# Moving the maxima's score matmuls behind the first half of a slot's fill work

## The chip, the cores and the metric

The kernel runs on one core of one Trainium2 chip. That core has five engines, each of which works through its own list of instructions in order: TensorE (PE, matrix products; its weight loads are listed as PEld), VectorE (DVE), ScalarE (ACT), GpSimd (POOL) and SyncE (SP, which here starts the DMA transfers). An engine waits for another by semaphores. The metric is the device time of one execution in microseconds (us); lower is better. A run of the kernel before takes 732.83 us as the median of three (732.78 to 732.90).

## The reference

Inputs are float32. `x` is 2048 by 512, the attention has 32 heads of width 16 and a sliding window of 256 keys, the MLP has 1792 hidden features.

```python
def _A_ref(x, wqkv, wo):
    qkv = (x @ wqkv).reshape(B, S, 3, H, Dh).transpose(2, 0, 3, 1, 4)
    q, k, v = qkv[0], qkv[1], qkv[2]
    scores = einsum("bhqd,bhkd->bhqk", q, k) * (Dh ** -0.5)
    mask = (idx[:, None] - idx[None, :] >= 0) & (idx[:, None] - idx[None, :] < W)
    p = softmax(where(mask, scores, -1e9), axis=-1)
    return einsum("bhqk,bhkd->bhqd", p, v).transpose(0, 2, 1, 3).reshape(B, S, D) @ wo

def _B_ref(x, w1, b1, w2, b2):
    h = gelu(layernorm(x) @ w1 + b1)
    return h @ w2 + b2

xn = layernorm(A_x)
return A_x + _A_ref(xn, wqkv, wo) * silu(_B_ref(xn, w1, b1, w2, b2))
```

## The kernel before

**Stages.** The first 60 us or so load the inputs, normalise and transpose `x` and make the first projections. Then comes the attention loop, and then the rest of the MLP, the output projection and the gating. The change is in the attention loop.

**Slots.** Heads are taken in 8 groups of 4, and the 2048 rows in 16 blocks of 128, which gives 16 x 8 = 128 slots, numbered by `t`. In slot `t` three things are done for three different blocks, one behind the other:

- `prob_block` makes the probabilities of block `t`, in two passes (`p` = 1, then `p` = 0). PE writes scores into the PSUM tile `stb` (2 matmuls of 384 columns, one for each half of the array's rows), ACT takes the exponential of them into an SBUF tile `pt`, and POOL masks the edges of `pt` with `affine_select`. There is one `stb`, so the second pass waits until ACT has read the first.
- `max_block` finds the row maxima of block `m = t + 12`, which are subtracted later. PE writes 4 matmuls of 256 columns into the PSUM tile `xy` ("the maxima's scores", for the block itself and the one before it). DVE then runs `copy_predicated`, which replaces the masked half of the diagonal block by the scores of the block two before ("first-block scores", in the PSUM tile `zo`), and a `tensor_reduce` with max over `xy` into `mt`. The first-block scores of block `m + 1` are made at the end of slot `t` by `first_scores`: 4 matmuls of 128 columns into `zo[:, :, 0:256]`. For a group's first two blocks there is nothing two before, and the copy takes a constant (`negc`) in place of `zo`.
- `pv_step` multiplies the probabilities of block `t - 1` with the values: 24 short matmuls into `otb`, which is `zo[:, 1, 256:384]`. Then a copy takes `otb` to SBUF (`oraw`). ACT makes this copy in most slots, and DVE in the last slot of a job (below).

`zo` spans two PSUM banks of 512 columns: `zo[:, 0]` and `zo[:, 1]`. The first-block scores lie in both, and `otb` lies in the second one.

**Fills.** The projections that later slots need are cut into units that fill PE's time between these steps. `tandem(t0, t1, one, two)` takes two such jobs (12 steps each, or 24 of half the width) and runs them as pairs of matmuls into the two banks `fb`, over the slots `t0` to `t1`: a first phase up to `mid`, then a second with the array's rows exchanged, and a last few units in slot `t1`, from which the results are copied out by ACT. In this text a job's slot `t0` is its *first slot*, `mid` its *middle slot* and `t1` its *last slot* (the list `ends_pair`); `t1 + 1` is often the next job's first slot. Each unit is put into the first or the second half of a slot (`fills[t, 0]`, `fills[t, 1]`). The first unit of the second phase has a set dependency on the latest copy of `otb`:

```python
tc.add_manual_dep(r.ins, outs["copy"].ins.name, ORDER, reason="the banks change rows")
```

**Order.** Every engine but SP keeps the order in which the program records its instructions. The main loop records, for a slot: the pass `p` = 1, `max_block`, the first half's fills, planned extra work, the pass `p` = 0, the second half's fills, the first-block scores of the next slot's block, and `pv_step`:

```python
if 0 < t < end:
    prob_block(t // 16, t % 16, 1)
if t >= 0 and m < end:
    max_block(m // 16, m % 16, m not in IN_PLACE)
fill_in(t, 0)
```

Waits between engines are derived from which instruction reads or writes which tile, and are attached to the instruction that has to wait; what stands behind it in its engine's list waits with it.

Of the kernel before, what the change touches and what calls it, by code (L numbers as in the profile page):

```python
# [26 lines left out]
LEAD = 12  # L27
# [23 lines left out]
def mixer_kernel(ctx, tc, x, wqk, wv, wo, w1, b1, w2, b2, out):  # L51
# [25 lines left out]
    def load(pool, tag, src, name, shape=(P, 512)):  # L77
        t = pool.tile(list(shape), F32, tag=tag, name=name)
        nc.sync.dma_start(t, src)
        return t  # L80
# [63 lines left out]
    def run(steps):  # L144
        for step in steps:
            step()
# [13 lines left out]
    def open_slot(i):  # L160
        slots.append(bigp.tile([P, 2, 2, S], F32R, tag=f"qk{i}", name=f"qk{i}"))
# [123 lines left out]
    fills = {}  # L285
    IN_PLACE = (LEAD,)
# [171 lines left out]
    taken, ends_pair = set(), set()  # L458
# [32 lines left out]
    def tandem(t0, t1, one, two, mid=None, back=None):  # L491

        n = one[0]
        lo, hi = slice(0, 64), slice(64, P)
        mid = mid or max(1, (t0 + t1 + 1) // 2)
        most = n // 4

        def places(slots, last):  # L500

            last = min(most, n // (len(slots) + 1)) if last else 0
            cuts = [(n - last) * k // len(slots) for k in range(len(slots) + 1)]
            out = []
            for t, a, b in zip(slots, cuts, cuts[1:]):
                ahead = min(b - a, n // 3) if t < 16 * NQ - LEAD else min(b - a, max(most, (b - a + 1) // 2))
                out += [(t, 0)] * ahead + [(t, 1)] * (b - a - ahead)
            return out + [(t1, 0)] * last

        first, second = places(range(t0, mid), False), places(range(back or mid, t1), True)  # L510
        for phase, where in enumerate((first, second)):
            for i in range(n):
                flags = dict(start=(phase == 0 and i == 0), stop=(phase == 1 and i == n - 1), skip_group_check=True)
                def unit(i=i, phase=phase, flags=flags):
                    made = ((two if phase == 0 else one)[1](fb[1 - phase], i, hi, **flags),
                            (one if phase == 0 else two)[1](fb[phase], i, lo, **flags))
                    if phase == 1 and i == 0 and t0 < 16 * NQ - LEAD:
                        for r in made:
                            tc.add_manual_dep(r.ins, outs["copy"].ins.name, ORDER, reason="the banks change rows")
                fills.setdefault(where[i], []).append((unit, ()))  # L520
        fills.setdefault((t1, 0), []).append((one[2], (fb[0], t1, nc.scalar.copy)))
        if t1 >= 16 * NQ - LEAD:
            fills[t1, 0].append((two[2], (fb[1], t1, nc.vector.tensor_copy)))
            return
        ends_pair.add(t1)

        def copy(dst, src):
            outs["second"] = nc.scalar.copy(dst, src)
        fills.setdefault((t1, 1), []).append((two[2], (fb[1], t1, copy)))
# [15 lines left out]
    def first_scores(n, qb):  # L545

        slot = slots[n % 2]
        for p in range(2):
            for a in (1, 0):
                r = slice(64 * a, 64 * a + 64)  # L550
                nc.tensor.matmul(zo[:, a, P * p: P * (p + 1)], slot[r, 0, p, P * qb: P * (qb + 1)],
                                 slot[r, 1, p, P * (qb - 2): P * (qb - 1)], start=True, stop=True)

    def max_block(n, qb, ahead=False):

        slot = slots[n % 2]
        if qb % 4 == 0:
            mts[n, qb // 4] = small.tile([P, 2, 2, 4], F32, tag="mt", name=f"mt_{n}_{qb}")
        lo = max(qb - 1, 0)
        off = 128 * (lo + 1 - qb)  # L560
        for p in range(2):
            for a in (1, 0):
                r = slice(64 * a, 64 * a + 64)
                nc.tensor.matmul(xy[:, a, 256 * p + off: 256 * (p + 1)], slot[r, 0, p, P * qb: P * (qb + 1)],
                                 slot[r, 1, p, P * lo: P * (qb + 1)], start=True, stop=True)
        if qb >= 2 and not ahead:
            first_scores(n, qb)
        four = xy.rearrange("q a (p k) -> q a p k", p=2)
        outs["max"] = nc.vector.copy_predicated(
            four[:, :, :, 128:256], mask,  # L570
            neg if qb < 2 else zo[:, :, 0:256].rearrange("q a (p k) -> q a p k", p=2)),
        nc.vector.tensor_reduce(out=mts[n, qb // 4][:, :, :, qb % 4],
                                in_=four[:, :, :, off:256],
                                axis=AX.X, op=ALU.max, negate=True)
# [32 lines left out]
    def prob_block(n, kb, p):  # L607
        slot = slots[n % 2]
        w = min(384, S - P * kb)
        pt = pp.tile([P, 2, 384], F32, tag="pt", name=f"pt_{n}_{kb}_{p}")  # L610
        both = xy if p and 16 * n + kb + LEAD >= 16 * NQ else stb[0]
        for a in (1, 0):
            r = slice(64 * a, 64 * a + 64)
            nc.tensor.matmul(both[:, a, 0:w], slot[r, 1, p, P * kb: P * (kb + 1)],
                             slot[r, 0, p, P * kb: P * kb + w], start=True, stop=True)
        writers[n, kb, p] = [nc.scalar.activation(pt[:, :, 0:w], both[:, :, 0:w], AF.Exp, scale=DH ** -0.5)]
        select = nc.gpsimd.affine_select(out=pt[:, :, 0:P], in_=pt[:, :, 0:P], pattern=[[0, 2], [1, P]],
                                compare_op=ALU.is_ge, fill=0.0, base=0, channel_multiplier=-1)
        if w == 384:
            select = nc.gpsimd.affine_select(out=pt[:, :, 256:384], in_=pt[:, :, 256:384],  # L620
                                             pattern=[[0, 2], [-1, P]], compare_op=ALU.is_gt, fill=0.0,
                                    base=0, channel_multiplier=1)
        writers[n, kb, p].append(select)
        pts[(n, kb, p)] = pt
# [122 lines left out]
    def at(t, fn, *args):  # L747
        plan.setdefault(t, []).append((fn, args))
# [8 lines left out]
    ahead = load(pp, "pt", x[512: 640, :], "x_1_0")  # L757
# [144 lines left out]
           -10: [ln3[0][0], ln3[1][0], ln3[0][1], ln3[1][1], ln3[0][2], ln3[1][2]],  # L902
           -9: [ln3[2][0], ln3[3][0], ln3[2][1], ln3[3][1], ln3[2][2], ln3[3][2]]}

    def fill_in(t, half):
        now[:] = t, half
        run(delayed.pop((t, half), ()))
        for fn, args in fills.get((t, half), ()):
            fn(*args)

    end = 16 * NQ
    for t in range(-16, end + 1):
        m = t + LEAD
        if t == -5:
            open_slot(1)
            for k in range(4):
                at(-4 + k // 2 * 2, clear_part, k)
        if 0 < t < end:
            prob_block(t // 16, t % 16, 1)
        if t >= 0 and m < end:  # L920
            max_block(m // 16, m % 16, m not in IN_PLACE)
        fill_in(t, 0)
        for fn, args in plan.get(t, []):
            fn(*args)
        if 4 <= m < LEAD:
            max_block(0, m)
        if 0 <= t < end:
            prob_block(t // 16, t % 16, 0)
        fill_in(t, 1)
        if t == -1:  # L930
            early.close()
            stb.append(attn.enter_context(tc.tile_pool(name="ps_s2", bufs=1, space=PSUM)).tile(
                [P, 2, 512], F32, name="stb"))
            prob_block(0, 0, 1)
            fill_in(t, 2)
        if 0 <= m < 4:
            max_block(0, m)
        if t >= 0 and m + 1 < end and (m + 1) % 16 >= 2 and m + 1 not in IN_PLACE:
            first_scores((m + 1) // 16, (m + 1) % 16)
        if t >= 1:  # L940
            pv_step((t - 1) // 16, (t - 1) % 16)
        run(lns.get(t, ()))
        if 0 <= m < end and m % 4 == 3:
            max_rows(m // 16, m % 16 // 4, t)
        for fn, args in ends.get(t, []):
            fn(*args)
# [28 lines left out]
    for f in range(6, NF, 2):  # L975
        t = gp.tile([P, 2, 512], F32, tag="ohl", name=f"hr_{f}", bufs=4)
# [199 lines left out]
    for c in range(2):  # L1176
# [25 lines left out]
        ahead = 2 + c  # L1202
# [4 lines left out]
        for i in range(NF + 1):  # L1207
# [29 lines left out]
            k = i - o_from  # L1237
# [190 lines left out]
```

## Time and profile before

| | us |
|---|---|
| median of 3 runs | 732.83 |
| the profiled execution, its own time | 732.75 |
| its span, first to last instruction | 731.0 |
| PE busy in the span | 719.0 |
| DVE busy | 497.9 |
| ACT busy | 427.0 |
| POOL busy | 321.3 |

The span is what the profile shows; 732.75 - 731.0 = 1.75 us of the run's time lie around it. Busy time of PE is counted from the start of a matmul to a modelled end, and matmuls overlap in the array, so PE can be "busy" while it moves slower than it could. What a step costs is therefore read from the distance between the starts of two steps that follow each other on PE. In the rows below a step is named by the tile that it writes: `stb` (probability scores), `xy` (the maxima's scores), `fb` (a fill), `zo<-qk` (first-block scores), `zo<-pt,vt` (`pv_step`). All instructions carry the line L43, that of the helper that records them, so they are told apart by tile.

### The profile page before, as it was taken

The page shows a single profiled execution, that of the slowest core. Times are in us where ns is not written, and L with a number is a line of the kernel's source. Part 1 is how long each engine was busy: PE and PEld are TensorE (multiplying, and loading weights), DVE is VectorE, ACT ScalarE, POOL GpSimd, SP SyncE. Part 2 cuts the span into 40 slices and gives each one's busy share as a digit, 9 for nine tenths or more (in the row PEclk, how much of TensorE's full clock was granted, in tenths as well). Part 3 has the DMA queues.
Part 4 walks back from the last instruction along what each step waited for, and adds up shares of the span by engine and source line. Part 5 has one row for each costly group of instructions (what it writes and reads, how often), then busy time and mean ns, then how long its engine had stood idle before and what let it go on. Part 6 is the DMA issues. An engine that isn't in the chain of part 4 may idle for free.

```text
span 731.0 us, 19063 instructions
## 1 busy us (share of the span) xinstructions
PE 719.0 (98%) x7584; PEld 585.9 (80%) x7584; DVE 497.9 (68%) x733; ACT 427.0 (58%) x723; POOL 321.3 (44%) x681
## 2 busy tenths in 40 slices
PE   8999999999999999999999999999999999999997
PEld 7997777777778887777776788888888888888886
DVE  7886776877766777777882657446787855667833
ACT  7767777877777676888878735232343734541001
POOL 7444757767677665777877540203203000001102
PEclk9999999999999999999999999999999999999999
DMA  8324446877776733667624367347213312263701
GB/s 294 82 48 105 101 126 171 223 217 226 206 209 171 210 121 97 161 165 212 176 78 159 130 220 203 143 130 244 87 57 116 117 58 87 66 190 109 247 22 58
DMA packets 61528, 106.77 MB, mean 146 GB/s; under 512 B 12096, under 2 KB 12352, under 8 KB 61440
## 3 DMA queue, kind: packets, MB, share of 16 engines
q1 hardware_dynamic: 61440, 105.56, 49.3%
q8 instruction: 60, 0.98, 0.5%
q14 instruction: 28, 0.23, 0.1%
HBM read 54.53 MB, written 33.82 MB: 121 GB/s over the span
## 4 chain that ended last, share of the span: by engine, by line
PE 93%; ACT 2%; DVE 2%; DMA 1%; SPq 1%; issue 1%; POOL 0%; DVEq 0%; ACTq 0%; POOLq 0%
PE acc L43 21%; PE fb L43 20%; PE zo L43 13%; PE p L43 9%; PE stb L43 9%; PE s L43 6%; PE h L43 6%; PE xy L43 5%; ACT pt L43 2%; PE pv L43 2%; SPq L43 1%; DMA wvr<-in_wv_dram 1%; DVE xy L43 0%; DVE mt L43 0%; DVE xnT L43 0%
## 5 line engine op out<-in xcount | busy, mean ns | idle before, releaser
L43 POOL TENSOR_SCALAR_AFFINE_SELECT pt<-pt 128x256 f32<-128x256 f32 x480 | 192.9, 426 | 97.5 <-ACT pt L43 91.5
L43 ACT ACTIVATE pt<-stb 128x768 f32<-128x768 f32 (+1 forms) x244 | 188.7, 773 | 44.5 <-PE stb L43 38.0
L43 DVE TENSOR_REDUCE mt<-xy 128x4 f32<-128x1024 f32 (+1 forms) x128 | 152.6, 1192 | 4.4
L43 DVE COPY_PREDICATED xy<-upper,zo 128x512 f32<-128x512 int32 x112 | 77.9, 695 | 73.8 <-PE xy L43 64.3
L43 POOL TENSOR_TENSOR xo<-xo,gated 128x512 f32<-128x512 f32 x15 | 19.9, 1330 | 221.3 <-DVE gated L43 220.3
L43 PE MATMUL zo<-pt,vt 128*17 128x128 f32 x2880 | 103.7, 275 | 0.0
L43 PE MATMUL fb<-xnT,wqb 64*128 64x512 f32 (+2 forms) x732 | 99.5, 381 | 0.1
L43 PE MATMUL stb<-qk 64*128 64x384 f32 (+1 forms) x488 | 94.6, 382 | 4.8 <-ACT pt L43 3.1
L43 PE MATMUL acc<-w,gh 128*128 128x512 f32 x320 | 98.5, 389 | 0.0
L43 PEld LDWEIGHTS stb<-qk 64*128 64x128 f32 x488 | 45.6, 183 | 48.1 <-ACT pt L43 39.3
L43 PEld LDWEIGHTS zo<-pt,vt 128*17 128x17 f32 x2880 | 67.5, 97 | 15.2 <-issue 4.9
L43 PEld LDWEIGHTS acc<-w,gh 128*128 128x128 f32 x320 | 60.1, 188 | 12.4
L43 PEld LDWEIGHTS fb<-xnT,wqb 64*128 64x128 f32 (+1 forms) x732 | 62.4, 185 | 7.0 <-ACT vt L43 0.3
L43 PE MATMUL acc<-w,gl 128*128 128x512 f32 x160 | 62.2, 389 | 0.0
L43 PE MATMUL xy<-qk 64*128 64x256 f32 (+2 forms) x536 | 58.1, 290 | 0.6 <-DVE mt L43 0.6
L43 PE MATMUL p<-xnT 128*128 128x512 f32 x189 | 51.8, 389 | 0.0
L43 PEld LDWEIGHTS xy<-qk 64*128 64x128 f32 x536 | 46.6, 185 | 5.5 <-issue 2.4
L43 ACT COPY oraw<-zo 128x128 f32<-128x128 f32 x108 | 28.7, 266 | 37.5 <-PE zo L43 28.8
L43 ACT ACTIVATE gated<-acc 128x512 f32<-128x512 f32 x16 | 8.7, 596 | 61.9 <-DVE acc L43 61.9
L43 PE MATMUL s<-wos,ohl 128*128 128x512 f32 (+1 forms) x204 | 44.3, 376 | 0.0
L43 PEld LDWEIGHTS s<-wos,ohl 128*128 128x128 f32 x204 | 36.8, 188 | 7.1
L43 PEld LDWEIGHTS p<-xnT 128*128 128x128 f32 x189 | 35.5, 188 | 7.4
(203 smaller groups left out, 1193.5 us busy)
## 6 DMA issues: line engine op xcount, KB each, us to landing
qk<-sh SPq DMA_DIRECT2D x128, 128.0 KB
qk<-pjr SPq DMA_DIRECT2D x64, 128.0 KB
oT_d<-oraw SPq DMA_DIRECT2D x32, 256.0 KB
w_d<-in_w_dram SPq DMA_DIRECT2D x14, 512.0 KB
xt_d<-xnT SPq DMA_DIRECT2D x12, 512.0 KB
x<-in_x_dram SPq DMA_DIRECT2D x16, 256.0 KB
w<-w_d SPq DMA_DIRECT2D x16, 256.0 KB
or<-oT_d SPq DMA_DIRECT2D x16, 256.0 KB
```

Source lines behind the costliest of these rows:

```text
L43: r = issue(*args, **kwargs)
```

## The change

Where a slot has fill units in its first half, `max_block` is recorded behind them and no longer ahead of them. `max_behind` counts these units and makes three exceptions at the end of the loop; slot 0 is another. The first-block scores change place around a job's end: in the last slot of a job they are made in that slot itself, straight ahead of its `max_block`, and in the slot behind it (mostly the next job's first) right behind the pass `p` = 1; the slots ahead of these two then no longer make them at their ends. In a job's first slot one unit more goes to the second half (`most` = 3 of 12 or 6 of 24 in the first half, and not 4 or 8). The number of instructions of each engine is the same, and so is the order on DVE, ACT, POOL and SP; on PE the order alone is changed.

```diff
@@ -504,6 +504,8 @@
             out = []
             for t, a, b in zip(slots, cuts, cuts[1:]):
                 ahead = min(b - a, n // 3) if t < 16 * NQ - LEAD else min(b - a, max(most, (b - a + 1) // 2))
+                if t == t0 > 3:
+                    ahead = min(ahead, most)
                 out += [(t, 0)] * ahead + [(t, 1)] * (b - a - ahead)
             return out + [(t1, 0)] * last
 
@@ -902,11 +904,27 @@
            -10: [ln3[0][0], ln3[1][0], ln3[0][1], ln3[1][1], ln3[0][2], ln3[1][2]],
            -9: [ln3[2][0], ln3[3][0], ln3[2][1], ln3[3][1], ln3[2][2], ln3[3][2]]}
 
-    def fill_in(t, half):
+    def max_behind(t, m):
+        units = sum(not args for _, args in fills.get((t, 0), ()))
+        if t == 0 or t == end - LEAD - 1:
+            return 0
+        return min(units, {end - LEAD - 2: 0, end - LEAD - 3: 2}.get(t, units))
+
+    def fill_in(t, half, ahead=None, m=None):
         now[:] = t, half
         run(delayed.pop((t, half), ()))
-        for fn, args in fills.get((t, half), ()):
+        for k, (fn, args) in enumerate(fills.get((t, half), ())):
+            if ahead and k == ahead:
+                own_max(t, m)
+                ahead = None
             fn(*args)
+        if ahead:
+            own_max(t, m)
+
+    def own_max(t, m):
+        if t in ends_pair and m % 16 >= 2:
+            first_scores(m // 16, m % 16)
+        max_block(m // 16, m % 16, m not in IN_PLACE)
 
     end = 16 * NQ
     for t in range(-16, end + 1):
@@ -917,9 +935,12 @@
                 at(-4 + k // 2 * 2, clear_part, k)
         if 0 < t < end:
             prob_block(t // 16, t % 16, 1)
-        if t >= 0 and m < end:
+        ahead = max_behind(t, m) if 0 <= t and m < end else None
+        if ahead == 0:
             max_block(m // 16, m % 16, m not in IN_PLACE)
-        fill_in(t, 0)
+        if t - 1 in ends_pair and m < end and m % 16 >= 2:
+            first_scores(m // 16, m % 16)
+        fill_in(t, 0, ahead, m)
         for fn, args in plan.get(t, []):
             fn(*args)
         if 4 <= m < LEAD:
@@ -935,7 +956,8 @@
             fill_in(t, 2)
         if 0 <= m < 4:
             max_block(0, m)
-        if t >= 0 and m + 1 < end and (m + 1) % 16 >= 2 and m + 1 not in IN_PLACE:
+        if (t >= 0 and m + 1 < end and (m + 1) % 16 >= 2 and m + 1 not in IN_PLACE
+                and not (t in ends_pair or t + 1 in ends_pair and max_behind(t + 1, m + 1))):
             first_scores((m + 1) // 16, (m + 1) % 16)
         if t >= 1:
             pv_step((t - 1) // 16, (t - 1) % 16)
```

## Prediction

> **What bounds the kernel now.** I read the page's busy times first, then the waits of the attention loop (70 to 386 us), then one slot in order of time.
>
> ```profile
> PE 719.0 (98%) x7584; PEld 585.9 (80%) x7584; DVE 497.9 (68%) x733; ACT 427.0 (58%) x723; POOL 321.3 (44%) x681
> ...
> DVE xy L43 <- PE xy L43: 75.3, 100, 1.4
> PEld stb L43 <- ACT pt L43: 38.8, 145, 0.9
> ...
> PEld zo L43 <- DVE xy L43: 3.3, 15, 0.4
> ```
>
> PE looks full. The waits (engine, tile, waited for; us in total, times, longest) say more: PE's loads wait for ACT 38.8 us in the loop, and for DVE's `xy` copy only 3.3 us. DVE is the engine with time to spare: it waits 75.3 us for the maxima's scores. Here is one ordinary slot (start, duration, engine, tile), on PE, then DVE, then ACT.
>
> ```profile
> 89.49 0.45 PE L43 MATMUL stb<-qk 64*128 64x384 f32 x2
> 89.77 0.40 PE L43 MATMUL xy<-qk 64*128 64x256 f32 x4
> 90.01 1.10 PE L43 MATMUL fb<-xnT,wqb 64*128 64x512 f32 x8
> 90.95 0.33 PE L43 MATMUL stb<-qk 64*128 64x384 f32 x2
> 91.12 0.34 PE L43 MATMUL zo<-qk 64*128 64x128 f32 x4
> 91.39 0.85 PE L43 MATMUL zo<-pt,vt 128*17 128x128 f32 x24
> 92.19 0.45 PE L43 MATMUL stb<-qk 64*128 64x384 f32 x2
> ...
> 90.27 0.70 DVE L43 COPY_PREDICATED xy<-upper,zo 128x512 f32<-128x512 int32 x1 [0.86 <-PE xy L43]
> 91.00 1.23 DVE L43 TENSOR_REDUCE mt<-xy 128x4 f32<-128x1024 f32 x1
> ...
> 89.72 0.27 ACT L43 COPY oraw<-zo 128x128 f32<-128x128 f32 x1 [0.29 <-PE zo L43]
> 89.98 0.81 ACT L43 ACTIVATE pt<-stb 128x768 f32<-128x768 f32 x1
> 91.33 0.81 ACT L43 ACTIVATE pt<-stb 128x768 f32<-128x768 f32 x1 [0.54 <-PE stb L43]
> 92.35 0.27 ACT L43 COPY oraw<-zo 128x128 f32<-128x128 f32 x1 [0.22 <-PE zo L43]
> ```
>
> The slot is 92.19 - 89.49 = 2.70 us long, and two chains of that length fit it. ACT's: scores, exponential (89.98 to 90.79), next scores, exponential (91.33 to 92.14), next slot, 1.35 us a pass. PE's: the steps from start to start are 0.28, 0.24, 0.94 (8 fills), 0.17, 0.27, 0.80. A third chain is hidden in it: from the start of the maxima's scores to DVE's copy 90.27 - 89.77 = 0.50, the copy 0.70, and only then the next first-block scores, since they overwrite what the copy reads. They start at 91.12, 0.15 behind the copy's end. Another slot shows the same order at a closer look:
>
> ```profile
> 202.63 0.69 DVE L43 COPY_PREDICATED xy<-upper,zo 128x512 f32<-128x512 int32 x1 [0.74 <-PE xy L43]
> 203.38 0.30 PEld L43 LDWEIGHTS zo<-qk 64*128 64x128 f32 x4
> 203.49 0.33 PE L43 MATMUL zo<-qk 64*128 64x128 f32 x4
> ```
>
> The copy ends at 203.32, the load starts 0.06 later and the matmul 0.17 later. So today the copy ends just when PE arrives: it costs PE nothing because the 0.94 us of fills stand between the maxima's scores and the first-block scores. **This cover is what the change takes away.**
>
> **The change, part by part.** No instruction is added or removed, so all cost is in waits. After the start of the maxima's scores, PE may not write `zo` for 0.50 + 0.70 + 0.15 to 0.17, I take 1.36 us. So far 0.24 + 0.94 + 0.17 = 1.35 us of its work lay in that time. Now only the scores and the pass lie there, 0.41 us, plus what the second half has of fills. Behind the matmul that waits stand `pv_step` and the next slot's first pass, so ACT's next exponential and POOL's masks wait with it.
>
> *Ordinary slots.* Pass 0.17 (the step 90.95 to 91.12, without a wait on ACT), 8 fills 0.94: the maxima's scores start at 1.11. First-block scores at 1.11 + 1.36 = 2.47, `pv_step` at 2.74, next slot at 3.54. ACT ends the second pass's exponential at 1.11 + 0.24 + 0.38 + 0.81 = 2.54, so it no longer bounds. Fills in the second half (0.23 a unit) vanish in the 1.36 us, so slots with them end at 3.54 too.
>
> *Middle slots.* The first fill waits for the latest `oraw` copy. It starts 0.16 to 0.23 into the slot (92.35, 89.72) and takes 0.27; until now the maxima's scores covered it. The first fill starts at about 0.58, not 0.17, and the slot is 3.95 long (two of them without first-block scores 3.68, one with the scores between its fills 3.48).
>
> *Slots ahead of a last slot, and last slots.* They no longer make first-block scores at their ends. But `pv_step` writes the second bank of `zo`, which the copy reads too, and it has a wait of its own.
>
> For PE, here is the end of slot 7 and the start of slot 8 (a job's last slot), before:
>
> ```order
> L43 MATMUL stb<-qk_94 128x384 [waits Activation_49]
> L43 MATMUL stb<-qk_94 128x384
> L43 MATMUL fb_111<-xnT,wqb_777 128x512
> L43 MATMUL fb_112<-xnT,wqb_777 128x512
> L43 MATMUL zo<-qk_751 128x128 [waits DMAHW4_49,DMAHW6_49,DMAHW2_49,DVE_49]
> L43 MATMUL zo<-qk_751 128x128 x3
> L43 MATMUL zo<-pt_4_0_1317,vt 17x128 x2
> ```
>
> and now, with the maxima's scores of slot 7 ahead of it:
>
> ```order
> L43 MATMUL xy<-qk_751 128x256 [waits DVE_49]
> L43 MATMUL xy<-qk_751 128x256 x3
> L43 MATMUL stb<-qk_94 128x384 [waits Activation_49]
> L43 MATMUL stb<-qk_94 128x384
> L43 MATMUL fb_111<-xnT,wqb_777 128x512
> L43 MATMUL fb_112<-xnT,wqb_777 128x512
> L43 MATMUL zo<-pt_4_0_1317,vt 17x128 [waits DVE_49]
> ```
>
> The first-block scores are gone from this place, and the wait for DVE has passed to `pv_step`. So it starts at 2.47 here too, and the slot ends at 3.27. In a last slot 6 fills (0.70) and the first-block scores (0.27) lie ahead of the maxima's scores, which start at 1.14; `pv_step` at 2.50, end 3.30.
>
> *First slots.* PE's list over the end of slot 8 and the start of slot 9 (a first slot) now reads:
>
> ```order
> L43 MATMUL zo<-pt_7_1_1432,vt 17x128 x2
> L43 MATMUL stb<-qk_94 128x384 [waits Activation_49]
> L43 MATMUL stb<-qk_94 128x384
> L43 MATMUL zo<-qk_751 128x128 [waits DVE_49]
> L43 MATMUL zo<-qk_751 128x128 x3
> L43 MATMUL fb_112<-xnT,wqb_1359 128x512 [waits Activation_49]
> ```
>
> The first-block scores have moved ahead of the fills, and what they wait for on DVE is the `oraw` copy, which in a last slot is DVE's and stands behind the reduce. On DVE the last slot has: copy 1.64 to 2.34, reduce 2.37 to 3.60, `oraw` about 3.62 to 3.91. That is 0.61 after the first slot's start. First-block scores at 0.78, 6 fills from 1.05, maxima's scores at 1.75, next first-block scores at 3.11, `pv_step` 3.38, end 4.18.
>
> The counts, and the length of all these slots today, come from the rows of `xy` and `zo` between 70 and 386 us (count, shortest/median/longest ns, first and last start):
>
> ```profile
> L43 PE MATMUL xy<-qk x452: 228/278/337, 70.4 to 384.6; 64*128 64x256 f32 x142, 64*128 64x128 f32 x9
> L43 DVE TENSOR_REDUCE mt<-xy x113: 692/1225/1228, 71.6 to 385.7; 128x4 f32<-128x1024 f32 x106, 128x4 f32<-128x512 f32 x7
> L43 DVE COPY_PREDICATED xy<-upper,zo x99: 660/696/697, 70.9 to 384.9; 128x512 f32<-128x512 int32 x99
> L43 DVE COPY_PREDICATED_SCALAR xy<-upper,negc x14: 753/754/755, 73.6 to 346.4; 128x512 f32 x14
> ...
> L43 ACT COPY oraw<-zo x94: 260/266/268, 70.2 to 384.3; 128x128 f32<-128x128 f32 x94
> L43 DVE COPY oraw<-zo x19: 280/292/294, 86.8 to 370.8; 128x128 f32<-128x128 f32 x19
> ```
>
> 452 / 4 = 113 slots, 112 steps, 384.6 - 70.4 = 314.2 us, 2.81 on average. In 14 the copy reads the constant and not `zo`, so nothing waits for it; of the other 99 the changed order spares the last two by its exceptions. That leaves 97, which I sort by the list of jobs in the code: 27 ordinary x 3.54 = 95.6; 19 middle = 16 x 3.95 + 2 x 3.68 + 3.48 = 74.0; 19 without first-block scores at their ends x 3.27 = 62.1; 16 last x 3.30 = 52.8; 16 first x 4.18 = 66.9. Sum 351.4. The other 15 of the 112 steps keep 2.81: 42.1. Together 393.5, which is 79.3 us more than 314.2. Made against the profiled execution's 732.75: **812 us**, and the median of the runs, 732.83, leads to the same. Outside the loop nothing is moved, so nothing is added. The DMA transfers have the same order and more time; each maximum is used 12 slots after it is made.
>
> **Bounds.** The 1.36 us come from two slots alone, so I give them 0.06 us either way: 97 x 0.06 = 6 us. The middle slots' wait is between nothing (the copy has ended) and 0.45: -8 to +1. The first slots' wait is between nothing and, if a transpose or a conversion stands ahead of the `oraw` copy on DVE, 0.5 more: 16 x 0.61 = -10 to +8. Waits of today that vanish in the new pauses cannot be more than ACT's extra passes in the 15 untouched slots, some 3 us, and I leave them out. Together 788 to 827 if all go one way.
>
> **Rivals.** *The second bank binds nobody.* If only overlapping columns counted, `pv_step` and the `oraw` copy would not wait: slots without first-block scores at their ends would end with ACT's pass at 2.60 (19 x -0.67), last slots at 2.62 (16 x -0.68), first slots 0.50 earlier: -13 - 11 - 8 = -32, so 780 us. Against it stands the wait of `pv_step` in the order quoted above. The Trainium skill speaks against it as well: its page "PSUM — Partial Sum Buffer", section "PSUM bank collisions raise a hardware error", says that two engines must be kept apart by bank and not by address. By that rule the forecast stands; no row here shows what happens without the wait.
>
> *Faster: the pauses do not come, and the waits of today go.* This is the other side. If PE reached the first-block scores no sooner than the copy ends, only gains were left: the 3.3 us of PE's waits for DVE's copy, which the new places at a job's end avoid. That gives 732.75 - 3.3 = 729.4 us. It decides for a gain only if 1.36 us of PE's work stand behind the maxima's scores; the ordinary slot has 0.41 there. The 27 ordinary slots alone, each 0.8 us longer by the sum above, speak against it.
>
> *PE's clock falls.* With pauses of about 0.9 us in each slot PE works 2.6 of 3.54 us, 73%. At half clock an ordinary slot's steps double (0.34, 1.88, then 1.36, 0.54, 1.60): 5.7 us, 2.2 more in 97 slots, some 1025 us. The nearest rows (length, busy us of PE, PEld, DVE, ACT, POOL, granted clock, DMA) are the program's start and the loop's:
>
> ```profile
> 0.00:9.00 9.00, 7.22 (x38) 6.59 (x38) 6.10 (x20) 6.51 (x6) 6.01 (x13) 1.00 0.74 239
> ...
> 60.00:66.00 6.00, 5.43 (x78) 4.48 (x74) 4.21 (x7) 3.42 (x6) 4.03 (x11) 1.00 0.58 125
> ```
>
> At 80% and 90% busy the clock is 1.00, and I expect it to stay. The Trainium skill ("TensorE: Matmul & The Clock Gate", Part 1) puts the fall at idle stretches of about 3.4 us, which no slot has here; the same page, in its section on depth-cycling, tells of a kernel whose short pauses made the clock swing, and by that the rival would hold.
>
> **How the numbers follow.** The forecast, pauses in nearly every slot and about 812 us, gets 0.90. The rival without the bank's waits 0.05 (780), the clock 0.02 (1025), faster 0.02 (729), and 0.01 for a time within 0.2% of now, where the pauses would just cancel what is won. 0.2% (1.5 us) is about what a measurement of this kernel can tell from no change. So faster 0.02, same 0.01, slower 0.97. The range is the bounds with a little of the rival below: 790 to 828 us.
>
> **What would show it.** In the changed profile PE's wait for DVE's `xy` copy should grow from 3.3 us in the loop to well over 50 us, spread over `zo<-qk` and `zo<-pt`; PE's loads should hardly wait for ACT's `pt` any more; ordinary slots should be 3.5 us from `stb` to `stb`, with the first-block scores 1.36 us behind the maxima's scores; first slots about 4.2, with the DVE `oraw` copy ending just before their first-block scores; and the span from 438 us on should be as long as before. The forecast is wrong if ordinary slots stay near 2.7 us, or if the granted clock is below 1.00.

## The result and the profile after

The changed kernel takes 805.73 us, the median of five runs (805.62 to 806.74), against 732.78 (732.62 to 732.90) of the kernel before on the same chip: a ratio of 1.0997, with a 95% interval of 1.0985 to 1.1010. It is 10% slower. The forecast was 812 us with a range of 790 to 828.

The page's busy times come first, then each engine's share of the chain that ended last.

```profile
PE 738.1 (92%) x7584; PEld 586.6 (73%) x7584; DVE 494.3 (61%) x733; ACT 427.6 (53%) x723; POOL 319.4 (40%) x681
...
PE 81%; DVE 10%; issue 4%; ACT 2%; DMA 2%; SPq 1%; DVEq 0%; ACTq 0%; POOL 0%; POOLq 0%
```

And the second of these rows as the page of the kernel before has it:

```profile
PE 93%; ACT 2%; DVE 2%; DMA 1%; SPq 1%; issue 1%; POOL 0%; DVEq 0%; ACTq 0%; POOLq 0%
```

The counts of instructions are the same. No engine is fuller than it was: every share fell, and PE at "92%" still looks like the bound. What changed is the chain. DVE, which has the time to spare, now makes 10% of it. Where the time went, the stretches show (start and end, length, busy us of PE, PEld, DVE, ACT and POOL, granted clock, DMA share, GB/s). After:

```profile
70.00:458.00 388.00, 329.58 (x4972) 246.91 (x4966) 229.34 (x289) 240.07 (x406) 222.33 (x531) 1.00 0.50 136
...
511.00:804.00 293.00, 289.21 (x1288) 239.87 (x1286) 184.20 (x304) 102.37 (x169) 32.58 (x23) 1.00 0.38 121
```

And before:

```profile
70.00:386.00 316.00, 311.13 (x4980) 246.75 (x4976) 232.06 (x289) 240.38 (x407) 226.31 (x533) 1.00 0.61 168
...
438.00:731.00 293.00, 289.31 (x1288) 239.87 (x1286) 185.02 (x304) 102.16 (x169) 31.48 (x23) 1.00 0.38 121
```

The attention loop is 72 us longer and the last 293 us are as they were. The clock is 1.00 in every stretch. In the loop PE was idle for 316.00 - 311.13 = 4.9 us and is now idle for 388.00 - 329.58 = 58.4. The other 72.0 - 53.5 = 18.5 us of the growth are counted as busy: ahead of a pause a group of matmuls is counted to its end (0.35 us for the second pass's scores, where the next step used to start 0.17 behind them), and the first-block scores behind the wait are shown longer (0.44 us in place of 0.34).

The waits in the loop (70 to 458 us; engine, tile, waited for, us in total, times, longest) name the cause:

```profile
PEld zo L43 <- DVE xy L43: 77.7, 94, 0.9
...
PE zo L43 <- DVE xy L43: 50.7, 89, 0.8
...
PEld zo L43 <- DVE oraw L43: 8.8, 16, 0.8
...
PEld stb L43 <- ACT pt L43: 5.1, 20, 0.4
```

PE's loads wait for DVE's `xy` copy 94 times, 77.7 us, where it was 15 times and 3.3 us; their wait for ACT's `pt` fell from 38.8 to 5.1. The new waits stand at about as many places as forecast, 94 of 97, and 16 more, one in each first slot, are for DVE's `oraw` copy.

One ordinary slot, in order of time (start, duration, engine, tile), PE, then DVE, then ACT:

```profile
93.12 0.45 PE L43 MATMUL stb<-qk 64*128 64x384 f32 x2
93.40 1.09 PE L43 MATMUL fb<-xnT,wqb 64*128 64x512 f32 x8
94.33 0.40 PE L43 MATMUL xy<-qk 64*128 64x256 f32 x4
94.56 0.35 PE L43 MATMUL stb<-qk 64*128 64x384 f32 x2
95.57 0.44 PE L43 MATMUL zo<-qk 64*128 64x128 f32 x4 [0.66 <-DVE xy L43]
95.94 0.85 PE L43 MATMUL zo<-pt,vt 128*17 128x128 f32 x24
96.72 0.44 PE L43 MATMUL stb<-qk 64*128 64x384 f32 x2
...
94.82 0.70 DVE L43 COPY_PREDICATED xy<-upper,zo 128x512 f32<-128x512 int32 x1 [1.65 <-PE xy L43]
...
94.95 0.81 ACT L43 ACTIVATE pt<-stb 128x768 f32<-128x768 f32 x1 [0.54 <-PE stb L43]
96.90 0.27 ACT L43 COPY oraw<-zo 128x128 f32<-128x128 f32 x1 [1.14 <-PE zo L43]
```

The slot is 96.72 - 93.12 = 3.60 us long. The maxima's scores start at 94.33, DVE's copy 0.49 later; it ends at 95.52, and the first-block scores start at 95.57. ACT has finished its exponential at 95.76 and then idles 1.14 us, where it was 0.22 before: the bound has passed from ACT and PE to the round trip PE, DVE, PE.

The first slot of a job, on PE, and DVE's `oraw` copy in it:

```profile
89.08 0.44 PE L43 MATMUL stb<-qk 64*128 64x384 f32 x2
89.76 0.44 PE L43 MATMUL zo<-qk 64*128 64x128 f32 x4 [0.24 <-DVE oraw L43]
90.03 0.90 PE L43 MATMUL fb<-xnT,wqb 64*128 64x512 f32 x6
...
89.42 0.28 DVE L43 COPY oraw<-zo 128x128 f32<-128x128 f32 x1
```

The `oraw` copy ends at 89.70 and the first-block scores start 0.06 later, with six fills queued behind them. The slot ends at 93.12: 4.04 us.

The lengths of all 112 steps, from the starts of the first pass's scores, sum up by the prediction's classes as follows:

| slots | count | before, us | forecast, us | after, us | after, mean of one |
|---|---|---|---|---|---|
| ordinary | 27 | 75.5 | 95.6 | 95.4 | 3.53 |
| middle | 19 | 52.7 | 74.0 | 71.9 | 3.78 |
| without first-block scores at the end | 19 | 53.7 | 62.1 | 60.9 | 3.20 |
| last | 16 | 43.7 | 52.8 | 51.0 | 3.19 |
| first | 16 | 46.1 | 66.9 | 65.5 | 4.09 |
| other | 15 | 42.4 | 42.1 | 42.3 | 2.82 |
| all | 112 | 314.1 | 393.5 | 387.0 | 3.46 |

The measured growth in length, 387.0 - 314.1 = 72.9 us, is that of the span, 803.9 - 731.0 = 72.9. So the loss lies in these slots and nowhere else.

### The profile page after: what moved, and what is told of

It is laid out like the page before. It is cut to its first block, busy times and chain, and to the rows that moved or that the text cites. A ratio compares the mean times of both kernels' runs of the same rounds, so it can differ in the third digit from the quotient of the medians.

```text
span 803.9 us, 19059 instructions
## 1 busy us (share of the span) xinstructions
PE 738.1 (92%) x7584; PEld 586.6 (73%) x7584; DVE 494.3 (61%) x733; ACT 427.6 (53%) x723; POOL 319.4 (40%) x681
## 4 chain that ended last, share of the span: by engine, by line
PE 81%; DVE 10%; issue 4%; ACT 2%; DMA 2%; SPq 1%; DVEq 0%; ACTq 0%; POOL 0%; POOLq 0%
PE acc L43 19%; PE fb L43 17%; PE zo L43 14%; PE p L43 8%; DVE xy L43 8%; PE s L43 5%; PE h L43 5%; PE xy L43 5%; PE stb L43 4%; PE pv L43 2%; SPq L43 1%; ACT pt L43 1%; DMA x<-in_x_dram 1%; ACT oraw L43 1%; DVE mt L43 1%
## 5 line engine op out<-in xcount | busy, mean ns | idle before, releaser
L43 POOL TENSOR_SCALAR_AFFINE_SELECT pt<-pt 128x256 f32<-128x256 f32 x480 | 187.7, 414 | 161.1 <-ACT pt L43 159.0
L43 ACT ACTIVATE pt<-stb 128x768 f32<-128x768 f32 (+1 forms) x244 | 188.5, 772 | 62.1 <-PE stb L43 57.2
L43 PE MATMUL zo<-qk 64*128 64x128 f32 x448 | 45.5, 282 | 35.0 <-DVE xy L43 29.3
L43 PEld LDWEIGHTS zo<-qk 64*128 64x128 f32 x448 | 34.9, 185 | 57.1 <-DVE xy L43 46.8
L43 PEld LDWEIGHTS fb<-xnT,wqb 64*128 64x128 f32 (+1 forms) x732 | 64.4, 185 | 10.4 <-ACT oraw L43 4.1
```

What stands on the lines that cost most here:

```text
L43: r = issue(*args, **kwargs)
```

## The experiments

All medians stand beside 732.8 to 732.9 us of the kernel before on the same chip. The diffs are against the changed kernel, but for the last one. The theory is that of the prediction: after the maxima's scores PE may not write `zo` until DVE's copy has read it, and the fills that covered this time are gone.

**The second part alone.** The maxima's scores stand ahead of the fills again; the first-block scores of last and first slots are made in these slots, ahead of the maxima's scores. `most` stays.

```diff
     def max_behind(t, m):
...
-        return min(units, {end - LEAD - 2: 0, end - LEAD - 3: 2}.get(t, units))
+        return 0
...
         if ahead == 0:
+            if (t in ends_pair or t - 1 in ends_pair) and m % 16 >= 2:
+                first_scores(m // 16, m % 16)
             max_block(m // 16, m % 16, m not in IN_PLACE)
-        if t - 1 in ends_pair and m < end and m % 16 >= 2:
-            first_scores(m // 16, m % 16)
...
         if (t >= 0 and m + 1 < end and (m + 1) % 16 >= 2 and m + 1 not in IN_PLACE
-                and not (t in ends_pair or t + 1 in ends_pair and max_behind(t + 1, m + 1))):
+                and not (t in ends_pair or t + 1 in ends_pair)):
             first_scores((m + 1) // 16, (m + 1) % 16)
```

> The maxima's scores ahead of the fills again in every slot; the first-block scores of last and first slots stay in these slots (ahead of the maxima's scores), and first slots keep one unit more in the second half. Theory (PE waits for DVE's copy because it starts late): the 0.94 us of fills cover the copy again, so about 733 us, 730 to 737, and PE's waits for DVE's xy copy back to a few us. Rival (the cost comes from the first-block scores' new places, with their wait for the oraw copy, and from the moved unit): still 750 us or more.

Measured: 743.3 us, ratio 1.0145 (1.0128 to 1.0162). The big loss is gone, as the theory has it, but 10.5 us remain that it did not expect, so the time lies above its range. A last slot of this kernel, on PE, then the load of its first-block scores, then ACT's `oraw` copy and second exponential in it:

```profile
83.94 0.44 PE L43 MATMUL stb<-qk 64*128 64x384 f32 x2
84.44 0.44 PE L43 MATMUL zo<-qk 64*128 64x128 f32 x4
...
85.00 0.86 PE L43 MATMUL fb<-xnT,wqb 64*128 64x512 f32 x6
...
87.25 0.44 PE L43 MATMUL stb<-qk 64*128 64x384 f32 x2 [0.38 <-ACT pt L43]
...
84.44 0.30 PEld L43 LDWEIGHTS zo<-qk 64*128 64x128 f32 x4 [0.31 <-ACT oraw L43]
...
84.12 0.27 ACT L43 COPY oraw<-zo 128x128 f32<-128x128 f32 x1 [0.27 <-PE zo L43]
...
85.90 0.58 ACT L43 COPY pjr<-fb 128x512 f32<-128x512 f32 x1 [0.66 <-PE fb L43]
86.38 0.82 ACT L43 ACTIVATE pt<-stb 128x768 f32<-128x768 f32 x1
```

Near the slot's start the first-block scores meet ACT's copy of `otb`: it ends at 84.39, their load waits for it, and they start at 84.44, 0.50 behind the first pass and not 0.28. They take 0.28 more ahead of the fills, so these end 0.5 later; ACT's copy of the fills' results (`pjr`), which stands in front of the second exponential, starts that much later too, and the next slot's scores wait for ACT. Last slots are 3.17 us on average (2.73 before), first slots 3.21 (2.88): 16 x 0.44 + 16 x 0.33 = 12.3 us. The slots ahead of a last one, which no longer make first-block scores, win back some 2 us (2.70 us on average and not 2.84), and no more, since ACT's two passes bound them. So the second part costs time by itself where the maxima's scores stand ahead of the fills.

**The first part alone.** The second part is undone: all first-block scores stand at the end of the slot before, and `most` is gone.

```diff
-                if t == t0 > 3:
-                    ahead = min(ahead, most)
...
     def own_max(t, m):
-        if t in ends_pair and m % 16 >= 2:
-            first_scores(m // 16, m % 16)
         max_block(m // 16, m % 16, m not in IN_PLACE)
...
-        if t - 1 in ends_pair and m < end and m % 16 >= 2:
-            first_scores(m // 16, m % 16)
...
         if (t >= 0 and m + 1 < end and (m + 1) % 16 >= 2 and m + 1 not in IN_PLACE
-                and not (t in ends_pair or t + 1 in ends_pair and max_behind(t + 1, m + 1))):
+):
             first_scores((m + 1) // 16, (m + 1) % 16)
```

> The maxima's scores behind the fills, everything else as in the kernel before. Theory: all slots but those whose copy reads the constant are 3.5 to 3.6 us, without the short slots ahead of a last slot (3.23 in the changed kernel) and without the long first slots (4.04): 17 x 0.37 + 16 x 0.3 - 16 x 0.44 = +4, so about 809 us, 802 to 816. Rival (the second part of the change carries the cost): 760 us or less.

Measured: 804.23 us, 1.0975 (1.0953 to 1.0997), within the theory's range. With the maxima's scores behind the fills and nothing else, 71.4 of the 72.9 us are there. What the second part wins in the slots ahead of a last one (3.20 us on average in place of 3.55) and in last slots (3.19, 3.28) it gives back in first slots (4.09, 3.57).

**Which part of `zo` binds.** Every slot makes its own first-block scores straight ahead of its maxima's scores, behind the fills, so that `pv_step` alone stands behind the wait. The rival from the prediction, by which only overwritten columns count, says that it does not wait, since it writes columns that the copy does not read.

```diff
     def own_max(t, m):
-        if t in ends_pair and m % 16 >= 2:
+        if t > 0 and m % 16 >= 2:
             first_scores(m // 16, m % 16)
...
         if ahead == 0:
+            if t > 0 and m % 16 >= 2 and m not in IN_PLACE:
+                first_scores(m // 16, m % 16)
             max_block(m // 16, m % 16, m not in IN_PLACE)
-        if t - 1 in ends_pair and m < end and m % 16 >= 2:
-            first_scores(m // 16, m % 16)
...
-        if (t >= 0 and m + 1 < end and (m + 1) % 16 >= 2 and m + 1 not in IN_PLACE
-                and not (t in ends_pair or t + 1 in ends_pair and max_behind(t + 1, m + 1))):
-            first_scores((m + 1) // 16, (m + 1) % 16)
```

> The changed kernel with every slot's first-block scores made in the slot itself, behind the fills and right ahead of its maxima's scores, so that they overwrite what a copy of the slot before has long read. Only pv_step, which writes other columns of the same bank, still stands behind this slot's copy. Theory (the wait goes by bank): pv_step waits 1.24 us behind the start of the maxima's scores, ordinary slots stay at 3.5 to 3.6 us, about 802 us, 795 to 812. Rival (only overwritten columns make PE wait): slots end with ACT's second pass at about 2.98 us, some 755 us.

Measured: 789.92 us, 1.078 (1.0758 to 1.0802). An ordinary slot on PE, and DVE's copy in it:

```profile
91.82 0.44 PE L43 MATMUL stb<-qk 64*128 64x384 f32 x2
...
93.01 0.34 PE L43 MATMUL zo<-qk 64*128 64x128 f32 x4
93.18 0.46 PE L43 MATMUL xy<-qk 64*128 64x256 f32 x4
...
94.49 0.85 PE L43 MATMUL zo<-pt,vt 128*17 128x128 f32 x24 [0.66 <-DVE xy L43]
95.27 0.44 PE L43 MATMUL stb<-qk 64*128 64x384 f32 x2
...
93.74 0.70 DVE L43 COPY_PREDICATED xy<-upper,zo 128x512 f32<-128x512 int32 x1 [1.49 <-PE xy L43]
```

`pv_step` starts 0.05 behind the copy's end at 94.44, although the columns differ. The rival's 755 us fall: it is not the overwritten columns alone that bind. Copy and `pv_step` share the bank, but also the tile `zo`, so this run does not tell whether the wait goes by bank or by tile. The time is below the theory's range too, since the expectation left out a gain: with their first-block scores behind the fills, first slots fell from 4.09 to 3.20 us on average, 16 x 0.89 = 14 us. The Trainium skill's page "PSUM — Partial Sum Buffer", in "PSUM bank collisions raise a hardware error", asks for guards by bank and not by address; this run and that of the second part alone, where it is ACT that reads the bank, agree with it as far as the waits go. What would happen without the wait was not tried.

**Without the wait for DVE's copy.** The copy reads the constant in all slots, so nothing needs to wait for it; the first-block scores are still made, but are left out of the maxima.

```diff
-            neg if qb < 2 else zo[:, :, 0:256].rearrange("q a (p k) -> q a p k", p=2)),
+            neg if qb < 2 or n or qb >= 12 else zo[:, :, 0:256].rearrange("q a (p k) -> q a p k", p=2)),
```

> The changed kernel, but DVE's copy takes the constant in every slot and no longer reads zo; the first-block scores are still computed and left out of the maxima. Theory: PE does not wait for the copy at all, ordinary slots fall to 2.7 us; what stays is the middle slots' wait (16 x 0.2) and the first slots' wait for DVE's oraw copy, which grows to 1.3 us since the last slots are shorter (16 x 1.3): 733 + 3 + 20 = 756 us, 748 to 766. Rival (the late scores cost by themselves, by the reduce or by ACT's chain): over 790 us.

Measured: 751.92 us, 1.0261 (1.0241 to 1.0282), within the theory's range. Of the loads' waits for DVE's `xy` copy this row is left between 70 and 380 us:

```profile
PEld zo L43 <- DVE xy L43: 0.4, 1, 0.4
```

This one wait is worth 805.73 - 751.92 = 53.8 us. Ordinary slots are 2.70 us again. They are no shorter than before, though nothing waits for the copy any more: ACT's two passes of 1.35 us remain. So even free of its wait the new order has nothing to win in them.

**And without DVE's `oraw` copy.** As the last one, and ACT makes the `oraw` copy in a job's last slot too.

```diff
-        by = nc.vector.tensor_copy if t in ends_pair else nc.scalar.copy
+        by = nc.scalar.copy
```

> As the run with the constant copy (zo not read by DVE, first-block scores left out of the maxima), and in addition ACT makes the oraw copy in every slot. Theory: then nothing on PE waits for DVE by way of zo; the first slots' wait goes from 1.2 to about 0.5 us, 10 x 0.7 + 6 x 0.9 = 12 less, while the last slots become bound by ACT (two exponentials, two copies, the oraw copy, 3.1 us, 16 x 0.35 = 5 more): about 744 us, 736 to 750. Rival (the last and first slots' cost is not the oraw copy's): 750 to 754 us.

Measured: 741.37 us, 1.0116 (1.0096 to 1.0136), within the theory's range, though not by its whole sum: last slots, which were to become bound by ACT, stay at 2.69 us. The first slot that took 3.91 us without this edit takes 3.36: its first-block scores start 0.65 behind the first pass, not 1.21. Even ACT's copy is late there (0.28 would be free of it). The time still lies 8.5 us above the kernel before: first slots are 9.4 us longer in sum, and middle slots 4.6 us, at 3.0 us each, since their first fill waits for the `oraw` copy; the other slots are 5 us shorter.

**Half the fills as cover.** The maxima's scores stand behind half of the first half's fills.

```diff
-        return min(units, {end - LEAD - 2: 0, end - LEAD - 3: 2}.get(t, units))
+        return min(units, {end - LEAD - 2: 0, end - LEAD - 3: 2}.get(t, units // 2))
```

> The changed kernel with the maxima's scores behind half of a first half's fills (2 of 4 units, 1 of 3) and not behind all. Theory (PE waits as long as the scores are late, less what lies behind them): ordinary slots 27 x 0.42, middle slots 19 x 0.62, first slots 16 x 0.7, last slots 16 x 0.17, those ahead of them nothing: 37 us over the kernel before, 770 us, 760 to 780; ordinary slots at 3.14 us. Rival (any fill ahead of them costs the whole wait): 795 us or more.

Measured: 764.76 us, 1.0435 (1.0414 to 1.0456), within the theory's range. An ordinary slot on PE:

```profile
90.79 0.45 PE L43 MATMUL stb<-qk 64*128 64x384 f32 x2
91.07 0.63 PE L43 MATMUL fb<-xnT,wqb 64*128 64x512 f32 x4
91.53 0.40 PE L43 MATMUL xy<-qk 64*128 64x256 f32 x4
91.77 0.63 PE L43 MATMUL fb<-xnT,wqb 64*128 64x512 f32 x4
...
92.78 0.44 PE L43 MATMUL zo<-qk 64*128 64x128 f32 x4 [0.20 <-DVE xy L43]
93.15 0.85 PE L43 MATMUL zo<-pt,vt 128*17 128x128 f32 x24
93.93 0.45 PE L43 MATMUL stb<-qk 64*128 64x384 f32 x2
```

From the maxima's scores to the first-block scores it is 1.25 us, as with all fills ahead (1.24), and 1.15 more to the slot's end. So the slot's length is the place of the maxima's scores + 2.39: 0.74 + 2.40 = 3.14 here, 1.21 + 2.39 = 3.60 in the changed kernel. At 0.28, where they stood before, it would be 2.67, just under the 2.70 that ACT's two passes need. For ordinary slots that is the whole change in one line.

**First slots' scores behind their fills.** In first slots the first-block scores stand behind the six fills, as in last slots, and not ahead of them.

```diff
     def own_max(t, m):
-        if t in ends_pair and m % 16 >= 2:
+        if (t in ends_pair or t - 1 in ends_pair) and m % 16 >= 2:
             first_scores(m // 16, m % 16)
...
-        if t - 1 in ends_pair and m < end and m % 16 >= 2:
-            first_scores(m // 16, m % 16)
```

> The changed kernel, but in the first slot of a job the first-block scores stand behind its 6 fills and not ahead of them. Theory (they wait there for DVE's oraw copy, which ends 0.6 us into the slot): the fills cover that wait, the maxima's scores start at 1.13 and not 1.70, a first slot goes from 4.04 to about 3.55 us, 16 x 0.49 = 8 us less: about 798 us, 794 to 802. Rival (the first slots are long because of their own copy alone): 804 to 807 us.

Measured: 796.82 us, 1.0872 (1.0856 to 1.0889), within the theory's range. The first slot on PE:

```profile
88.67 0.44 PE L43 MATMUL stb<-qk 64*128 64x384 f32 x2
88.95 0.85 PE L43 MATMUL fb<-xnT,wqb 64*128 64x512 f32 x6
89.64 0.33 PE L43 MATMUL zo<-qk 64*128 64x128 f32 x4
```

No wait for the `oraw` copy is left here, and in the whole loop a single one of 0.2 us: the fills cover it. The slot is 92.20 - 88.67 = 3.53 us long (4.04 in the changed kernel); 16 x 0.51 = 8.2 of the 8.9 us.

**The other direction.** If behind the fills is too late, earlier might be better. This is the kernel before with `max_block` ahead of the first pass.

```diff
+        if t >= 0 and m < end:
+            max_block(m // 16, m % 16, m not in IN_PLACE)
         if 0 < t < end:
             prob_block(t // 16, t % 16, 1)
-        if t >= 0 and m < end:
-            max_block(m // 16, m % 16, m not in IN_PLACE)
```

> The kernel before, with the maxima's scores moved the other way, ahead of the slot's first pass, into the time in which PE waits for ACT's exponential. Theory (the copy only has to be done when PE comes to the first-block scores, and ACT's two passes of 1.35 us set the slot): nothing to gain in ordinary slots, up to 0.1 us in those with fills in their second half: 731 us, 727 to 736. Rival (the sooner the copy starts the better): under 725 us.

Measured: 747.22 us, 1.0196 (1.0179 to 1.0213), a miss. The timeline of this kernel, a second pass and the slot behind it, PE and ACT:

```profile
92.50 0.45 PE L43 MATMUL stb<-qk 64*128 64x384 f32 x2
...
93.83 0.50 PE L43 MATMUL xy<-qk 64*128 64x256 f32 x4
...
94.17 0.34 PE L43 MATMUL stb<-qk 64*128 64x384 f32 x2
...
92.99 0.81 ACT L43 ACTIVATE pt<-stb 128x768 f32<-128x768 f32 x1 [0.54 <-PE stb L43]
...
94.55 0.81 ACT L43 ACTIVATE pt<-stb 128x768 f32<-128x768 f32 x1 [0.27 <-PE stb L43]
```

The pass's scores now come 0.34 behind the maxima's scores. ACT's exponential starts 94.55 - 92.99 = 1.56 us after the one before it, and not 1.35. The slot is 93.83 - 90.91 = 2.92 us long (the maxima's scores of the slot before start at 90.91), against 2.70. The expectation gave DVE more room, and left out that ACT, the other chain of 2.70 us, has none. So of the places tried the one of the kernel before is the best, and no version here beats it.

## Why the prediction was right

**The bound and the mechanism** were right. The cover named in the prediction, 0.94 us of fills between the maxima's scores and the first-block scores, was what held DVE's round trip off the path. Taking the wait away (the copy that reads a constant) and halving the cover each give the time that this theory expects.

**The 1.36 us** were right in sum and not in their split. From the maxima's scores to `pv_step` the forecast had 1.36 + 0.27 = 1.63; measured are 1.24 + 0.37 = 1.61. The scores start 0.05 behind the copy, not 0.15, and `pv_step` comes 0.10 later behind them, since the loads stood in the pause too (load and matmul both start at 95.57, where the load used to start 0.11 ahead). The maxima's scores start at 1.21 and not 1.11: the first pass keeps its 0.28. So a typical ordinary slot is 3.60 and not 3.54, and the ±0.06 was too narrow for the 1.36 alone, which measured 1.24. That the class of ordinary slots came out within 0.2 us of its sum is luck: the 0.06 in 27 slots is offset by the term that follows.

**The term that was mis-sized** is the count of `pv_step`'s matmuls. The prediction charged 24 in every slot. In the two slots where a group of heads begins there are 8 and 16, as these rows of the changed kernel show:

```profile
228.60 0.44 PE L43 MATMUL stb<-qk 64*128 64x384 f32 x2
...
231.42 0.41 PE L43 MATMUL zo<-pt,vt 128*17 128x128 f32 x8
231.76 0.44 PE L43 MATMUL stb<-qk 64*128 64x384 f32 x2
...
234.58 0.63 PE L43 MATMUL zo<-pt,vt 128*17 128x128 f32 x16
235.14 0.44 PE L43 MATMUL stb<-qk 64*128 64x384 f32 x2
```

These slots are 3.16 and 3.38 us long, not 3.60. Before, ACT's 2.70 hid the difference; once PE sets the end it counts: 7 x 0.44 + 6 x 0.22 = 4.4 of the 6.5 us by which the sum was too high (a seventh slot with 16 is among the 15 that were left at 2.81).

**Middle, last and first slots** had the right order and the right waits, each a little shorter: typical middle slots 3.92 (forecast 3.95), last and ahead-of-last slots 3.22 and 3.23 (3.30 and 3.27), first slots 4.04 (4.18), where the first-block scores start at 0.68 and not 0.78. Together this is 0.5 + 1.3 + 0.8 + 2.2 = 4.8 us, which the longer ordinary slots (27 x 0.06 = 1.6) and two first slots of 4.36 and 4.37 us partly give back.

**The rivals.** That the second bank binds nobody: fallen, since `pv_step` waits for the copy, and the first-block scores for ACT's `oraw` copy, in columns that do not meet. That only gains are left: fallen; even without the wait ordinary slots are 2.70 us, so there was nothing to win. PE's clock: 1.00 in every stretch, with pauses of 0.66 us in a slot of 3.60. The Trainium skill's page "TensorE: Matmul & The Clock Gate", Part 1, puts the fall at an idle stretch of about 3.4 us; no pause here comes near it, the longest wait of PE in the loop being 0.8 us. What its section on depth-cycling tells of another kernel, that short pauses made the clock swing, was not seen in this one.

**What stays open:** the share of each wait is known only by taking them away one behind the other, and shorter slots make the next wait longer (in first slots the `oraw` copy held the first-block scores to 0.68 in the changed kernel, and to 1.21 without the `xy` wait). So 53.8 us for the copy is its worth in this order of removal, not a part of an exact sum. Whether PE's waits go by bank or by the whole tile `zo` stays open too.

## What to carry to other kernels

Before an instruction is moved, look at what it hands to another engine and when its own engine next needs that tile or its bank back; the work between the two is cover, and a full engine with hardly any waits can hide such a round trip of just its length. A move that shortens the cover costs, slot for slot, what the round trip then sticks out, until another chain bounds. Where two chains are both as long as the slot, here ACT's passes and PE's steps, neither earlier nor later was better, and a count that the longer chain hid (8, 16 or 24 matmuls) has to be taken up again as soon as the other one sets the end.

## What the runs showed of the hardware

Two things had not been expected. A wait in front of a step costs behind it too: from the start of the four first-block matmuls to that of `pv_step` it is 0.37 us where they wait, and 0.27 where they do not. And PE's busy share tells of pauses only in part: the loop grew by 72 us, but 18.5 of these are shown as busy, so that PE reads 85% in the loop (329.58 of 388.00 us) and 92% over the span, in a kernel whose slots in the loop nearly all end by a wait for DVE.
